# Four products in one half's inverse transform, another split of copies, more input buffers and earlier table loads in a convolution kernel

## The chip, the cores and the metric

The kernel runs on one core of a Trainium2 chip. The metric is the device time of one execution in microseconds (us). Five engines work side by side: PE (TensorE, matrix products), DVE (VectorE), ACT (ScalarE), POOL (GpSimd), and SP, which here only issues transfers (DMAs).

## The reference

Three parts follow each other: a long convolution with a gate, then two feed-forward layers over the 12480 tokens of 128 channels. All is float32.

```python
h_mlp = np.maximum(pos_emb @ w1, 0.0) @ w2            # filter, 12480 x 128
h_filt = h_mlp * np.exp(-0.01 * pos)[:, None]
u = x * v
y = irfft(rfft(u, n=2 * S) * rfft(h_filt, n=2 * S))[:S]   # along the tokens
x = x * y
h = x @ w_in; P = a0 + a1*h + a2*h**2 + a3*h**3; Q = 1 + |b0|*|h| + |b1|*h**2
x = (P / (Q + 1e-06)) @ w_out                         # 128 -> 2048 -> 128
out = np.maximum(0.01 * g, g) @ w_out2, with g = x @ w_in2
```

## The kernel before

The convolution is a Fourier transform over n = n1 * 128 + n2, made of matrix products in two stages, and taken apart into two halves of 64 channels (g = 0 and g = 1). After it come the two feed-forward layers, whose instructions a planner has put in order. The change leaves the planner's part alone; it takes from 400 us to the end of the span. What lies ahead of it runs in this order:

**Filter and u** (to about 106 us). PE, ACT and DVE compute the filter's network; ACT copies it to `hf` (half 0) and by way of DRAM (`hsc`) keeps half 1. In between stand 16 calls of `make_u(c)`: POOL multiplies a chunk of x by one of v (98 x 1024 elements), then DVE makes the sum and the difference of mirrored rows, two instructions of 98 x 512 that write the array `u`. The chunks come through `XB` = 4 buffers for x and `VB` = 2 for v; `load_u` puts the next loads into SP's queue, four DMAs for a chunk of x and four for a chunk of v, two of each four of 192 KB. Each DMA on SP or ACT also waits for an earlier one, since the program's DMAs take eight semaphores in turn.

**First stage, half 0.** `first(g, s, i)`, 16 chunks for the filter (s = 1) and 16 for u (s = 0). A chunk is four products (eight matrix instructions) into one of three PSUM buffers (`ps_b`), and a copy out of it into `A`. ACT copies in three instructions (L644 to L646), except for the chunks that the table `DCH` names for that (g, s): those are copied by DVE in four (L640 to L642). A chunk's products wait until the chunk three before it has been copied. Between the chunks stands `feed(1)`: one step of `conv_all`, which turns the float64 weights of the layers into float32. A weight chunk takes six DVE instructions (L586 to L601), then two on POOL (L605, L608), then a store by SP (`wsc`). Six steps are one weight chunk.

**Second stage, half 0.** 23 blocks. `second(b)`: products `xp` on PE with a table `mt` that SP loads from `c_m`; ACT copies the filter's part (L678); DVE multiplies twice (L685); POOL makes the complex product's parts in `yt`, index 2 and 1 (L691, L692), and their sum, index 0 (L693). Three blocks later `inverse(b)`: three products `gp` with the three tables in `em`, into the single PSUM buffer of `ps_s`; ACT copies the common part to `g1` (L706), DVE adds it to both others into `gs` (L708, two buffers), and SP stores `gs` to DRAM (`bd`). After each block come two steps of `conv_all`.

**First stage and second stage, half 1.** The same for the other 64 channels. The last three inverse blocks of half 0 stand among the first chunks of `first(1, 0, i)`. There too POOL brings half 1 of the filter into `hf` in four copies (L768), and these can't start before the last `bd` stores have read the memory that `hf` shares. The first three tables for half 1 (`early`) are loaded by SP at chunks 13 to 15 of `first(1, 1, i)`.

## Time and profile before

| | |
|---|---|
| median of 3 runs (lowest to highest) | 1721.95 us (1721.27 to 1724.23) |
| the profiled execution: time, span | 1720.13 us, 1718.3 us |
| PE busy in the span | 93% |
| DVE, ACT, POOL busy in the span | 88%, 81%, 83% |
| mean granted TensorE clock | 0.974 of full speed |

The span runs from the first to the last instruction of the profiled execution; 1.8 us of its time lie outside. Times in the rows below are in us from the span's start unless a column says ns.

### The profile page before, as it was taken

What the parts mean: (1) busy time and instruction counts of PE and PEld (TensorE: products, weight loads), DVE (VectorE), ACT (ScalarE), POOL (GpSimd) and SP (SyncE); (2) the same over time, 40 slices, a digit from 0 to 9 for tenths busy, and PEclk for the clock granted to TensorE, in tenths of its full rate; (3) what the DMA queues carried; (4) which work ended last, traced back from release to release, by engine and by line L of the source; (5) the groups of instructions that cost most, each with busy time, mean ns of one, the idle gap of its engine ahead of it and who ended that gap; (6) DMA issues with size and microseconds to landing.
All of it is one profiled execution on the core that took longest, in us unless ns stands there. A gap on an engine that the chain in (4) does not pass through costs nothing.

```text
span 1718.3 us, 21544 instructions
## 1 busy us (share of the span) xinstructions
PE 1604.1 (93%) x6394; PEld 1122.3 (65%) x6394; DVE 1507.3 (88%) x2473; ACT 1385.0 (81%) x2651; POOL 1424.1 (83%) x1209
## 2 busy tenths in 40 slices
PE   7648777987999999999999999999999999999999
PEld 4537667864566666666666666666666666666666
DVE  3488887658999999999999999999999999999992
ACT  4424235337999999999999999999999999999995
POOL 4535772748999999999999999999999999999993
PEclk9969998988999999999999999999999999999999
DMA  6734832761111110111110111110011111010000
GB/s 168 219 120 140 246 132 80 244 172 25 26 30 30 26 30 6 35 30 31 30 26 10 30 30 30 35 27 23 12 30 35 30 31 26 5 30 5 5 5 15
DMA packets 90100, 97.13 MB, mean 57 GB/s; under 512 B 53290, under 2 KB 58416, under 8 KB 89142
## 3 DMA queue, kind: packets, MB, share of 16 engines
q1 hardware_dynamic: 87462, 92.65, 19.8%
q10 hardware_dynamic: 2520, 3.09, 0.6%
q8 instruction: 51, 0.84, 0.2%
q14 instruction: 67, 0.55, 0.1%
HBM read 70.65 MB, written 25.07 MB: 56 GB/s over the span
## 4 chain that ended last, share of the span: by engine, by line
PE 80%; DVE 7%; DMA 5%; POOL 3%; issue 3%; ACT 2%; SPq 0%; ACTq 0%; POOLq 0%; DVEq 0%
PE o1p L964 19%; PE o2p L964 14%; PE h L489 11%; PE h L490 10%; PE h L491 10%; PE yP L919 3%; PE ap L635 3%; PE xp L676 2%; PE gp L702 1%; DMA bd<-wk 1%; PE o2p L491 1%; PE o2p L490 1%; PE o2p L489 1%; DMA hsc<-A 1%; PE oP L1041 1%
## 5 line engine op out<-in xcount | busy, mean ns | idle before, releaser
L1000 POOL TENSOR_TENSOR wk<-wk 128x980 f32<-128x980 f32 (+1 forms) x208 | 471.3, 2266 | 57.3 <-DVE wk L997 55.8
L964 PE MATMUL o1p<-g,wo 128*128 128x490 f32 (+1 forms) x832 | 386.6, 573 | 9.4 <-DVE g L1015 9.1
L991 POOL TENSOR_SCALAR wk<-wk,pars 128x490 f32<-128x490 f32 (+1 forms) x416 | 312.3, 752 | 49.0 <-ACT wk L983 45.2
L1002 DVE SCALAR_TENSOR_TENSOR v<-wk,absb,v 128x490 f32<-128x490 f32 (+1 forms) x416 | 298.7, 718 | 21.4 <-ACT v L985 14.6
L1009 DVE SCALAR_TENSOR_TENSOR v<-v,r 128x490 f32<-128x490 f32 (+1 forms) x416 | 275.1, 663 | 30.1 <-ACT r L1007 27.7
L964 PE MATMUL o2p<-wk,wo 128*128 128x490 f32 (+1 forms) x624 | 299.4, 568 | 0.0
L1005 ACT ACTIVATE rho<-v,cone 128x490 f32<-128x490 f32 (+1 forms) x416 | 279.9, 674 | 7.0 <-DVE v L1002 5.1
L1012 DVE SCALAR_TENSOR_TENSOR v<-v,r 128x490 f32<-128x490 f32 (+1 forms) x416 | 268.7, 662 | 4.3
L997 DVE TENSOR_TENSOR wk<-h,wk 128x490 f32<-128x490 f32 (+1 forms) x416 | 271.6, 653 | 0.5
L985 ACT ACTIVATE v<-h,absb 128x490 f32<-128x490 f32 (+1 forms) x416 | 254.6, 646 | 19.3 <-DVE g L1015 13.4
L1022 ACT ACTIVATE wk<-h 128x490 f32<-128x490 f32 (+1 forms) x416 | 241.9, 582 | 27.2 <-PE h L491 12.5
L1015 DVE TENSOR_TENSOR g<-wk,v 128x490 f32<-128x490 f32 (+1 forms) x416 | 254.0, 650 | 6.6 <-POOL wk L1000 6.1
L1007 ACT ACTIVATE r<-rho 128x490 f32<-128x490 f32 (+1 forms) x416 | 255.9, 617 | 4.5
L489 PE MATMUL h<-zh,wh 128*128 128x490 f32 (+1 forms) x416 | 248.6, 598 | 4.6 <-DVE wk L997 2.6
L983 ACT ACTIVATE wk<-h 128x490 f32<-128x490 f32 (+1 forms) x416 | 239.8, 579 | 15.9 <-PE h L491 12.6
L993 POOL TENSOR_SCALAR wk<-wk,pars 128x980 f32<-128x980 f32 (+1 forms) x208 | 239.0, 1149 | 0.0
L489 PE MATMUL h<-uh,wh 128*128 128x490 f32 (+1 forms) x416 | 226.4, 544 | 2.1 <-ACT wk L1022 1.3
L964 PEld LDWEIGHTS o1p<-g,wo 128*128 128x128 f32 x832 | 156.8, 191 | 105.0 <-issue 49.9
L491 PE MATMUL h<-zh,wl 128*128 128x490 f32 (+1 forms) x416 | 160.4, 386 | 0.0
L490 PE MATMUL h<-zl,wh 128*128 128x490 f32 (+1 forms) x416 | 160.2, 385 | 0.0
L490 PE MATMUL h<-ul,wh 128*128 128x490 f32 (+1 forms) x416 | 159.1, 382 | 0.0
L491 PE MATMUL h<-uh,wl 128*128 128x490 f32 (+1 forms) x416 | 159.0, 382 | 0.0
(100 smaller groups left out, 2522.5 us busy)
## 6 DMA issues: line engine op xcount, KB each, us to landing
bd<-wk SPq DMA_DIRECT2D x44, 256.0 KB
wk<-c_m SPq DMA_DIRECT2D x43, 256.0 KB
bt<-bd SPq DMA_DIRECT2D x96, 112.5 KB
dt<-c_d SPq DMA_DIRECT2D x24, 344.5 KB
A<-x SPq DMA_DIRECT2D x32, 192.0 KB
A<-v SPq DMA_DIRECT2D x32, 192.0 KB
out<-ot SPq DMA_DIRECT2D x32, 192.0 KB
xc<-x SPq DMA_DIRECT2D x24, 240.0 KB
```

Of the source, the lines that this page charges most:

```text
L489: pe.matmul(dst, w_h, z_h, start=start, stop=False)
L490: pe.matmul(dst, w_h, z_l, start=False, stop=False)
L491: pe.matmul(dst, w_l, z_h, start=False, stop=stop)
L964: pe.matmul(o, wo[l][:, f], T.pop((src, n))[:, :w], start=(f == 0), stop=(f == NF - 1))
L991: pool.tensor_scalar(out=q, in0=sq, scalar1=a3, scalar2=a1, op0=ALU.mult, op1=ALU.add)
L997: dve.tensor_tensor(out=half("nn"), in0=one("h1"), in1=two("q"), op=ALU.mult)
L1000: pool.tensor_tensor(out=nn, in0=nn, in1=T["p", n][:, : 2 * w], op=ALU.add)
L1002: dve.scalar_tensor_tensor(out=one("v"), in0=two("s"), scalar=bb, in1=one("v"), op0=ALU.mult, op1=ALU.add)
L1005: act.activation(mk("rho"), one("v"), AF.Abs_reciprocal_sqrt, bias=cone)
L1007: act.activation(mk("r0"), one("rho"), AF.Square)
L1009: dve.scalar_tensor_tensor(out=one("v"), in0=one("v"), scalar=C1, in1=one("r0"), op0=ALU.add, op1=ALU.mult)
L1012: dve.scalar_tensor_tensor(out=one("v"), in0=one("v"), scalar=-2.0, in1=one("r0"), op0=ALU.add, op1=ALU.mult)
```

## The change

Five things. (1) In half 0 the inverse is four products instead of three: real and imaginary part are each the sum of two products in PSUM. The sum `yt` index 0 is not made there (L693), and neither is DVE's addition: ACT copies both parts straight into `gs`. Half 1 keeps the three products; its tables are loaded into `em` between the halves. (2) `DCH` names 15 chunks for DVE instead of 24, so ACT copies 49 of 64. (3) x has six buffers and v four; those for v move to memory that `conv_all` uses later. (4) DVE's sum and difference in `make_u` go through the elements in the order in which x and v lie, and write `u` with a step of 128 elements; before, the reads had that step, and four elements in a row were written. (5) The three early tables are loaded at chunks 0 to 2 of `first(1, 1, i)`.

```diff
-    e = np.stack([np.cos(a), -np.sin(a) - np.cos(a), np.sin(a) - np.cos(a)], axis=1)
+    e = np.stack([
+        np.cos(a), np.sin(a), -np.sin(a), np.cos(a), -np.sin(a) - np.cos(a), np.sin(a) - np.cos(a)
+    ]).reshape(2, 3, N2, N2).transpose(0, 2, 1, 3)
...
-        XB, VB = 4, 2
+        XB, VB = 6, 4
         XS = [cut(Aw, AH + i * 2 * UB * D, [2, UB, D]) for i in range(XB)]
-        VS = [cut(Aw, AH + (XB + i) * 2 * UB * D, [2, UB, D]) for i in range(VB)]
+        VS = [cut(wk, N2 * DG + i * 2 * UB * D, [2, UB, D]) for i in range(VB)]
...
-                dve.tensor_tensor(
-                    out=u[:NU, :, j : j + UB], in0=t[:, 1].rearrange("p n d -> p d n"),
-                    in1=t[:, 0, ::-1].rearrange("p n d -> p d n"), op=alu,
-                )
+                dve.tensor_tensor(out=un[:NU, j : j + UB], in0=t[:, 1], in1=t[:, 0, ::-1], op=alu)
...
-        sp.dma_start(em, I["c_e"])
+        sp.dma_start(em, I["c_e"][0])
...
         DCH = {
-            (0, 1): (4, 6, 8, 10, 12, 14), (0, 0): (1, 4, 6, 9, 11, 14),
-            (1, 0): (1, 4, 6, 9, 11, 14), (1, 1): (1, 4, 6, 9, 11, 14),
+            (0, 1): (9, 12, 15), (0, 0): (2, 6, 10, 14), (1, 0): (2, 6, 10, 14), (1, 1): (2, 6, 10, 14),
         }
...
-                en.tensor_tensor(out=yt[:, 0, :kn], in0=yt[:, 1, :kn], in1=yt[:, 2, :kn], op=ALU.add)
+                if g:
+                    en.tensor_tensor(out=yt[:, 0, :kn], in0=yt[:, 1, :kn], in1=yt[:, 2, :kn], op=ALU.add)
...
-                for r in (2, 1, 0):
-                    pe.matmul(gp[:, r + (r > 0), :kn], em[:, r], yt[:, r, :kn], start=True, stop=True)
+                if g:
+                    for r in (2, 1, 0):
+                        pe.matmul(gp[:, r + (r > 0), :kn], em[:, r], yt[:, r, :kn], start=True, stop=True)
+                else:
+                    for r, es in ((0, (0, 2)), (1, (1, 0))):
+                        for i, e in enumerate(es):
+                            pe.matmul(gp[:, 2 + r, :kn], em[:, e], yt[:, 2 - i, :kn], start=(i == 0), stop=(i == 1))
...
-                    g1 = view("g1", [KB, DG])
-                    act.copy(g1[:, :kn], gp[:, 0, :kn])
                     gs = view("mt" if g and b > NB - 3 else "gs", [KB, 2, DG])
-                    dve.tensor_tensor(
-                        out=gs[:, :kn].rearrange("p k r d -> p r k d"), in0=gp[:, 2:4, :kn],
-                        in1=g1[:, :kn].unsqueeze(1).to_broadcast([128, 2, kn, DG]), op=ALU.add,
-                    )
+                    dst = gs[:, :kn].rearrange("p k r d -> p r k d")
+                    if g:
+                        g1 = view("g1", [KB, DG])
+                        act.copy(g1[:, :kn], gp[:, 0, :kn])
+                        dve.tensor_tensor(
+                            out=dst, in0=gp[:, 2:4, :kn],
+                            in1=g1[:, :kn].unsqueeze(1).to_broadcast([128, 2, kn, DG]), op=ALU.add,
+                        )
+                    else:
+                        act.copy(dst, gp[:, 2:4, :kn])
...
             first(1, 1, i)
+            if i < NE:
+                early[i] = cut(uw, 3072 + 512 * i, [KB, 128])
+                fetch_m(early[i], i)
+            if i == NE:
+                sp.dma_start(em, I["c_e"][1])
             feed(1)
-            if i >= 16 - NE:
-                b = i + NE - 16
-                early[b] = cut(uw, 3072 + 512 * b, [KB, 128])
-                fetch_m(early[b], b)
```

Three places of DVE's program show what moves. The first is the end of `make_u` and the start of its copies in the first stage of half 0; in `ap_1_16` the second number is the channel at which the chunk starts (chunk 4). Before:

```order
5 L476 TENSOR_TENSOR u<-A 98x128x4 x32
6 L640 COPY A<-ap_1_16_612 64x90x4 x2
7 L641 COPY A<-ap_1_16_612 64x90x4
8 L642 TENSOR_SCALAR A<-ap_1_16_612 64x90x4
9 L586 TENSOR_SCALAR wk<-wk 128x512
10 L588 TENSOR_SCALAR wk<-wk 128x512
11 L640 COPY A<-ap_1_24_633 64x90x4 x2
```

The same place in the changed kernel:

```order
5 L479 TENSOR_TENSOR u<-A 98x4x128 x32
6 L586 TENSOR_SCALAR wk<-wk 128x512
7 L588 TENSOR_SCALAR wk<-wk 128x512
8 L591 TENSOR_SCALAR wk<-wk 128x512
9 L595 TENSOR_SCALAR wk<-wk 128x512
10 L597 SCALAR_TENSOR_TENSOR wk<-wk 128x512
11 L640 COPY A<-ap_1_36_663 64x90x4 x2
12 L641 COPY A<-ap_1_36_663 64x90x4
13 L642 TENSOR_SCALAR A<-ap_1_36_663 64x90x4
```

DVE's first copy after u is now chunk 9 instead of chunk 4, and five weight steps stand ahead of it. The second place is three blocks of the second stage of half 0, DVE before:

```order
75 L708 TENSOR_TENSOR wk<-gp_0_944,wk 128x2x4x64
76 L685 TENSOR_TENSOR wk<-xp_3_938,wk 128x512 x2
77 L586 TENSOR_SCALAR wk<-wk 128x512
78 L588 TENSOR_SCALAR wk<-wk 128x512
79 L708 TENSOR_TENSOR wk<-gp_1_967,wk 128x2x4x64
80 L685 TENSOR_TENSOR wk<-xp_4_961,wk 128x512 x2
81 L591 TENSOR_SCALAR wk<-wk 128x512
82 L595 TENSOR_SCALAR wk<-wk 128x512
83 L708 TENSOR_TENSOR wk<-gp_2_988,wk 128x2x4x64
84 L685 TENSOR_TENSOR wk<-xp_5_982,wk 128x512 x2
85 L597 SCALAR_TENSOR_TENSOR wk<-wk 128x512
86 L601 SCALAR_TENSOR_TENSOR wk<-wk 128x512
```

And in the changed kernel:

```order
60 L684 TENSOR_TENSOR wk<-xp_3_934,wk 128x512 x2
61 L586 TENSOR_SCALAR wk<-wk 128x512
62 L588 TENSOR_SCALAR wk<-wk 128x512
63 L684 TENSOR_TENSOR wk<-xp_4_956,wk 128x512 x2
64 L591 TENSOR_SCALAR wk<-wk 128x512
65 L595 TENSOR_SCALAR wk<-wk 128x512
66 L684 TENSOR_TENSOR wk<-xp_5_976,wk 128x512 x2
67 L597 SCALAR_TENSOR_TENSOR wk<-wk 128x512
68 L601 SCALAR_TENSOR_TENSOR wk<-wk 128x512
```

The additions that read `gp` are gone from DVE, and the weight steps keep their places. The third place is DVE at the start of the first stage of half 1 (`ap_0_4`, `ap_0_16` and `ap_0_24` are chunks 1, 4 and 6). Before, from chunk 4:

```order
165 L640 COPY A<-ap_0_16_1442 64x90x4 x2
166 L641 COPY A<-ap_0_16_1442 64x90x4
167 L642 TENSOR_SCALAR A<-ap_0_16_1442 64x90x4
168 L601 SCALAR_TENSOR_TENSOR wk<-wk 128x512
169 L586 TENSOR_SCALAR wk<-wk 128x512
170 L640 COPY A<-ap_0_24_1467 64x90x4 x2
171 L641 COPY A<-ap_0_24_1467 64x90x4
172 L642 TENSOR_SCALAR A<-ap_0_24_1467 64x90x4
173 L588 TENSOR_SCALAR wk<-wk 128x512
174 L591 TENSOR_SCALAR wk<-wk 128x512
175 L595 TENSOR_SCALAR wk<-wk 128x512
176 L640 COPY A<-ap_0_36_1496 64x90x4 x2
```

In the changed kernel, from chunk 6 (`ap_0_24`) to chunk 10 (`ap_0_40`):

```order
125 L597 SCALAR_TENSOR_TENSOR wk<-wk 128x512
126 L601 SCALAR_TENSOR_TENSOR wk<-wk 128x512
127 L586 TENSOR_SCALAR wk<-wk 128x512
128 L640 COPY A<-ap_0_24_1442 64x90x4 x2
129 L641 COPY A<-ap_0_24_1442 64x90x4
130 L642 TENSOR_SCALAR A<-ap_0_24_1442 64x90x4
131 L588 TENSOR_SCALAR wk<-wk 128x512
132 L591 TENSOR_SCALAR wk<-wk 128x512
133 L595 TENSOR_SCALAR wk<-wk 128x512
134 L597 SCALAR_TENSOR_TENSOR wk<-wk 128x512
135 L640 COPY A<-ap_0_40_1480 64x90x4 x2
```

The steps L588 and L591 stood ahead of chunk 9's copy, and now stand, with L595 and L597, ahead of chunk 10's.

## Rows read from the trace of the kernel before

**Rows 1.** Windows: length, busy us (count) of PE, PEld, DVE, ACT, POOL, clock, DMA share, GB/s

```profile
145.00:240.00 95.00, 76.81 (x337) 62.09 (x336) 77.63 (x121) 23.60 (x49) 69.83 (x81) 0.98 0.65 205
297.00:372.00 75.00, 72.36 (x318) 61.73 (x318) 50.54 (x84) 26.64 (x58) 49.60 (x66) 0.96 0.61 207
400.00:1718.00 1318.00, 1298.70 (x4955) 867.14 (x4954) 1233.12 (x2062) 1231.40 (x2346) 1204.72 (x1002) 1.00 0.10 23
```

**Rows 2.** Timeline, 66 to 144 us: start, length, instruction, idle time before and its releaser

```profile
66.49 2.35 POOL L472 TENSOR_TENSOR A<-A 98x1024 f32<-98x1024 f32 x1 [3.18 <-DMA A<-v]
...
78.09 4.48 POOL L472 TENSOR_TENSOR A<-A 98x1024 f32<-98x1024 f32 x1
...
106.32 0.95 DVE L640 COPY A<-ap 64x360 f32<-64x360 f32 x2
...
108.30 0.43 DVE L586 TENSOR_SCALAR wk<-wk 128x512 int32<-128x512 int32 x1
108.33 7.31 PE L635 MATMUL ap<-f1t,wk 128*128 128x180 f32 x32 [27.81 <-DVE A L642]
...
143.71 7.14 PE L676 MATMUL xp<-A,wk 128*128 128x256 f32 x32 [1.72 <-ACT A L646]
```

**Rows 3.** Waits of SP's queue, 34 to 64 us, then 64 to 99: total, times, longest

```profile
SPq L347 <- DMA hsc<-A: 18.2, 10, 6.8
...
SPq L347 <- DVE u L476: 6.1, 4, 2.8
```

**Rows 4.** DVE's line L476, 66 to 107 us: ns shortest/median/longest

```profile
L476 DVE TENSOR_TENSOR u<-A x18: 1114/1222/3186, 68.9 to 105.2; 98x512 f32<-98x512 f32 x18
```

**Rows 5.** Instruction groups up to 374 us: busy us, mean ns, idle before

```profile
L803 DVE TENSOR_TENSOR wl<-w2f,wh 128x512 fp32r<-128x512 f32 x8 | 5.5, 681 | 0.0
...
L708 DVE TENSOR_TENSOR wk<-gp,wk 128x512 f32<-128x512 f32 x44 | 30.1, 687 | 16.9 <-ACT wk L706 9.0 <-DMA bd<-wk 7.5
...
L644 ACT COPY A<-ap 64x720 f32<-64x720 f32 x40 | 30.1, 752 | 74.4 <-PE ap L635 70.6 <-DMA hsc<-A 3.4
...
L646 ACT ACTIVATE A<-ap 64x360 f32<-64x360 f32 x40 | 18.6, 465 | 0.0
L645 ACT COPY A<-ap 64x360 f32<-64x360 f32 x40 | 18.1, 454 | 0.5
```

**Rows 6.** Timeline of PE, second stage: half 0 three and six blocks on, then half 1

```profile
168.53 1.53 PE L702 MATMUL gp<-wk,em 128*128 128x256 f32 x6 [0.27 <-DVE wk L708]
...
179.98 1.53 PE L702 MATMUL gp<-wk,em 128*128 128x256 f32 x6 [0.27 <-DVE wk L708]
...
314.74 1.89 PE L676 MATMUL xp<-A,wk 128*128 128x256 f32 x8
...
316.47 1.46 PE L702 MATMUL gp<-wk,em 128*128 128x256 f32 x6
...
317.76 1.89 PE L676 MATMUL xp<-A,wk 128*128 128x256 f32 x8
```

**Rows 7.** Waits, 143 to 236 us: total, times, longest

```profile
PE gp L702 <- DVE wk L708: 17.8, 16, 3.6
...
DVE wk L708 <- DMA bd<-wk: 7.5, 6, 3.6
```

**Rows 8.** DMA traffic, 172 to 215 us

```profile
DMA packets 4302, 10.61 MB, mean 247 GB/s; under 512 B 496, under 2 KB 496, under 8 KB 3973
```

**Rows 9.** Timeline, 238 to 300 us, first stage of half 1

```profile
239.34 0.94 PE L702 MATMUL gp<-wk,em 128*128 128x128 f32 x6
...
244.16 7.82 POOL L768 COPY wk<-u 82x2048 f32<-82x2048 f32 x2 [9.87 <-DMA bd<-wk]
...
257.91 3.95 DVE L591 TENSOR_SCALAR wk<-wk 128x512 int32<-128x512 int32 x1
...
264.34 7.59 PE L635 MATMUL ap<-f,u 98*128 98x180 f32 x32 [3.71 <-DVE A L642]
...
297.41 2.90 PE L676 MATMUL xp<-A,u 128*128 128x256 f32 x6 [3.96 <-DMA u<-c_m]
```

More of the change, by code (lines that the diff above doesn't have):

```diff
@@ L407, in conv_moe_moe @@
         un = u.rearrange("p d n -> p n d")
-        rh = cut(Aw, AH + 3 * 2048, [N2 // 2, NH])
+        rh = cut(Aw, AH + 6 * 1024, [N2 // 2, NH])
         pos = cut(Aw, 0, [N2, FO])
```

## The prediction

> **What bounds the kernel now.** I read the windows first, cut by stage. From 400 us on PE is busy for 1298.7 of 1318 us at the full granted clock [rows 1]; the change touches nothing there, so that part stays. Everything that can move lies ahead of it. In the second stage of half 0 PE is at 76.8 of 95 us and DVE at 77.6, in that of half 1 PE is at 72.4 of 75 [rows 1]: the same work is set by PE in half 1 and by something else in half 0. Then I followed the chain that ends each stage in the timeline, which gives four stretches.
>
> *u.* POOL starts chunk 7 at 66.49, and DVE is done with the last chunk and turns to the first copy at 106.32 [rows 2]. A lone product on POOL takes 2.35 us; the one at 78.09, which starts while DVE works on the chunk before, takes 4.48 [rows 2]. DVE's instruction takes 1.11 us at its shortest and up to 3.19 [rows 4]. So the two hold each other up: nine chunks in 39.83 us are 4.43 each, about 2.35 + 2 x 1.11 = 4.57. They run one behind the other all the way, and PE stands idle for 27.8 us behind them [rows 2], because the copy of chunk 4 is queued on DVE behind u.
>
> *First stage, half 0.* From 108.33 to the first `xp` at 143.71 [rows 2] it does 25 chunks, 1.415 us each.
>
> *Second stage, half 0.* 143.71 [rows 2] to the last `gp` at 239.34 [rows 9], 95.6 us. In its steady part three blocks take 179.98 - 168.53 = 11.45 us, 3.82 a block; a block of half 1 takes PE 1.73 us (`xp`) and 1.29 (`gp`), 3.02 [rows 6]. PE waits 17.8 us for DVE's addition L708, and that in turn 7.5 us for the store of the buffer it writes to [rows 7]: DVE is the bound, the stores add to it.
>
> *First stage, half 1.* 239.34 to 297.41, 58.1 us. POOL's copies start at 244.16; meanwhile DVE's weight steps, such as L591 at 257.91, take 3.95 us where L586 alone takes 0.43 [rows 2, 9]. Chunk 6 waits on DVE behind them, so PE goes on with chunk 9 only at 264.34. At the end PE waits 3.96 us for the early tables [rows 9].
>
> **The change part by part.**
>
> *Buffers for x and v.* I cost them at nothing. Between 34 and 64 us SP waits for no buffer, only for DMAs ahead, 18.2 us of it for stores of `hsc` [rows 3]; more buffers leave that as it is. After 64 us it waits 6.1 us for DVE to free one [rows 3], but that is hidden under POOL and DVE, which are the bound there. If that cover goes, loads have to bring 4 x 192 KB = 0.79 MB a chunk, 3.2 us at the 247 GB/s of [rows 8].
>
> *The new order of DVE's sum and difference.* No row shows a DVE write of single elements 512 bytes apart. With operands that lie in order, 128x512 from SBUF takes 0.681 us (L803, [rows 5]), against 1.114 for L476. The copy L640 writes runs of four elements, 512 bytes apart, at 0.95 / 2 = 0.475 us for 360 elements [rows 2], no slower per element than L803, so the steps between runs cost nothing. I take 0.681, since the strided reads are what sets L476 apart from both. Two instructions in nine chunks: 9 x 2 x 0.433 = 7.8 us. A chunk then takes 3.56 us, just above the 3.2 of the loads. Bounds: 0 if writes with that step cost what such reads do, 9 x (4.43 - 3.2) = 11 if only the loads were left. u ends at 98.5.
>
> The Trainium skill (Advanced Engine Details and Errata, SBUF Cachelines) says that accesses which move to another 16-byte line each time are penalised, and names no difference of reads and writes. L476's reads agree with it, at 1.114 against 0.681 us. By that rule the new writes, one element to a line, would keep the instruction near 1.11 us, and the 7.8 us would fall away.
>
> *Copies in the first stage of half 0.* ACT now takes chunks 0 to 8 before u is done, which needs 9 x (0.752 + 0.454 + 0.465) = 15 us [rows 5], well inside PE's 27.8 us of idling. After u, DVE has five weight steps (5 x 0.43 = 2.2 us), then chunk 9 (106.32 to 108.30, 1.98 us [rows 2]), and PE resumes at chunk 12 with 20 left: 2.2 + 2.0 + 20 x 1.415 = 32.5, against 143.71 - 106.32 = 37.4. Gain 4.9. ACT has three chunks in four, 5.0 us for 4 x 1.415 = 5.7. Bounds 3 (steps held up by the weight load) to 8 (1.27 us a chunk, the rate after 264.34, below).
>
> *Four products.* PE pays 1.29 / 3 = 0.43 us more a block: 1.73 + 1.72 = 3.45. DVE loses L708, 0.687 us [rows 5]: 11.45 - 3 x 0.687 = 9.4 us for three blocks, below PE's 10.35. POOL loses one of three instructions. ACT copies 512 instead of 256 elements a block, hidden: it was busy 23.6 of 95 us [rows 1]. So PE becomes the bound. 22.5 blocks (the last is half) x 3.45 = 77.6, and three first-stage chunks in between at 1.27 are 3.8: 81.4 against 95.6, at best 14.2. Transfers take some of it back: 172 to 215 us moves 10.61 MB at 247 GB/s [rows 8], and at PE's pace (3.45 for about 4.1 us a block) that would need 290. I take 3 us off: gain 11.2. Lower bound 5: that stretch stays as it is, and the other 52.6 us shrink by 1 - 10.35 / 11.45.
>
> *Copies in the first stage of half 1.* DVE has L597, L601 and L586 before POOL's copies start, then chunk 6 in time; L588 needs POOL's L608, which stands behind two of the four copies, so chunk 10 now takes the place that chunk 6 had, behind the copies. PE does four chunks more before it stops there, and resumes at chunk 13 instead of 9. From 264.34 to the end of the products (297.41 - 3.96 = 293.45) 23 chunks took 1.27 us each [rows 9]; so 4 x 1.27 = 5.1, less 0.7 for L597, the one step more ahead of the copy. Gain 4.4; bounds 2 and 10, where the copies collide otherwise.
>
> *Early tables.* They leave SP's queue behind chunks 0 to 2, ahead of the last two weight stores. PE waits 3.96 us for them, of which the copy of the last chunk (1.67 us, L644 to L646 [rows 5]) stays: gain 2.3. The half's `em` goes out with them, a dozen chunks before it is read, and costs nothing; were it late, the first `gp` of half 1 would wait.
>
> Sum: 7.8 + 4.9 + 11.2 + 4.4 + 2.3 = 30.6 us. The profiled execution took 1720.13, span 1718.3 and 1.8 around it, so 1689.5; the median of the runs is 1.8 above that execution, which gives 1691.4.
>
> **The rivals.**
>
> *Writes cost as reads did* (the rule above, as a mechanism of this kernel): u again ends near 106.3, and 22.8 us are left: 1699. For it: the nearest row has runs of four, not single elements. Against: L640 shows no cost of its writes.
>
> *Transfers bound the second stage of half 0.* `gs` has two buffers; DVE already waits 7.5 us for their stores [rows 7], and at 3.45 us a block the time for a store to land shrinks from 8 to 7 us. Then ACT waits in L708's place and holds PE's single `gp` buffer. Against: half 1 runs at 3.02 with the same buffers and 207 GB/s [rows 1, 6]. It leaves the lower bound: 1720.13 - 30.6 + 6.2 + 1.8, 1698; with the rival above, 1705.
>
> *Slower.* The new writes are far dearer than the reads. Place: L479, 18 instructions after 66 us, each with POOL kept out. From (1.11 + 22.8 / 18) = 2.4 us for one, twice what it takes now, they eat all other gains; at 3 us the kernel is at about 1733. For it: no row with such writes. Against: the slowest undisturbed access here is 1.114.
>
> *The change doesn't do what it says:* the deeper buffers load nothing earlier, as [rows 3] show for 34 to 64 us. That is in the sum already.
>
> **How the numbers follow.** Likeliest, 0.5: 1691.4, own range 1684 to 1698. Writes as dear as reads, 0.26: 1699. Transfers, 0.12: 1698; both, 0.05: 1705. Slower, 0.03: 1733. Better than 1683 (bounds of several terms at once), 0.04. The range 1683 to 1706 leaves out the last two and the edges. 0.2% is 3.4 us, about what a measurement can tell from no change: faster 0.95, the same 0.02, slower 0.03.
>
> **What would show it.** L479 near 0.68 us, and DVE's first copy near 98.5. First `xp` near 131. In half 0's second stage `gp` to `gp` 3.45 us with PE busy throughout; waits there for a `bd` store speak for the transfers. POOL's copies still stretch L588 and L591, and PE resumes at chunk 13 right after. The first `xp` of half 1 follows ACT's last copy, not a DMA. The prediction is wrong if L479 stays above 1 us, or if the 1318 us of the layers move.

## The result, and the profile after

The changed kernel takes 1696.38 us (median of 4 runs, 1694.75 to 1704.04) against 1721.87 for the kernel before, measured beside it: a ratio of 0.9858, 95% interval [0.9827, 0.9889]. It is 25.5 us faster. 1691.4 was forecast, with a range of 1683 to 1706. The profiled execution took 1696.18 us, with a span of 1694.4, 23.9 less than before.

The timeline of the changed kernel gives the marks that cut the 23.9 us into stages (start, length, instruction, idle time before and its releaser):

```profile
67.43 2.35 POOL L475 TENSOR_TENSOR A<-A,wk 98x1024 f32<-98x1024 f32 x1 [3.01 <-DMA wk<-v]
...
89.38 1.49 PE L635 MATMUL ap<-f1t,wk 128*128 128x180 f32 x8 [1.68 <-ACT A L646]
92.54 1.49 PE L635 MATMUL ap<-f1t,wk 128*128 128x180 f32 x8 [1.68 <-ACT A L646]
...
103.06 0.41 DVE L586 TENSOR_SCALAR wk<-wk 128x512 int32<-128x512 int32 x1
...
107.00 2.77 PE L635 MATMUL ap<-f,u 98*128 98x180 f32 x8 [12.97 <-DVE A L642]
111.74 7.94 PE L635 MATMUL ap<-f,u 98*128 98x180 f32 x32 [1.98 <-DVE A L642]
120.14 13.98 PE L635 MATMUL ap<-f,u 98*128 98x180 f32 x88 [0.46 <-ACT A L646]
135.84 7.14 PE L675 MATMUL xp<-A,wk 128*128 128x256 f32 x32 [1.72 <-ACT A L646]
...
169.40 1.89 PE L707 MATMUL gp<-wk,em 128*128 128x256 f32 x8
...
172.85 1.89 PE L707 MATMUL gp<-wk,em 128*128 128x256 f32 x8
...
223.72 1.06 PE L707 MATMUL gp<-wk,em 128*128 128x128 f32 x8
...
227.32 7.66 POOL L777 COPY wk<-u 82x2048 f32<-82x2048 f32 x2 [10.37 <-DVE wk L601]
...
240.85 3.86 DVE L591 TENSOR_SCALAR wk<-wk 128x512 int32<-128x512 int32 x1
...
247.79 6.94 PE L635 MATMUL ap<-f,u 98*128 98x180 f32 x24 [10.52 <-DVE A L642]
254.57 20.26 PE L635 MATMUL ap<-f1t,wk 128*128 128x180 f32 x128
276.51 5.45 PE L675 MATMUL xp<-A,u 128*128 128x256 f32 x24 [1.68 <-ACT A L646]
...
283.52 1.46 PE L703 MATMUL gp<-wk,em 128*128 128x256 f32 x6
```

On PE, x8 of L635 is one chunk of a first stage; `f1t` marks the filter's chunks and `f,u` those of u. Five marks of each kernel do for the whole study: POOL's chunk 7 (67.43 here), the end of u (DVE's next step, 103.06), the first `xp` (135.84), the last `gp` of half 0 (223.72, the 128x128 one), and the first `xp` of half 1 (276.51). Before, they stood at 66.49, 106.32, 143.71, 239.34 and 297.41 [rows 2, 9]. Differences of such marks, from the timeline of each kernel's profiled execution, in us:

| kernel | chunk 7 to end of u | to first `xp` | to last `gp` | to `xp` of half 1 | to the end |
|---|---|---|---|---|---|
| before | 39.83 | 37.39 | 95.63 | 58.07 | 1420.89 |
| changed | 35.63 | 32.78 | 87.88 | 52.79 | 1417.89 |
| changed, once more (e11) | 35.85 | 32.05 | 88.86 | 51.95 | 1418.51 |
| e1 u in a row | 32.01 | 32.02 | 91.61 | 52.05 | 1418.73 |
| e2 three `gs` | 36.07 | 32.20 | 87.15 | 52.86 | 1420.98 |
| e3 steps later | 35.44 | 32.00 | 87.86 | 47.91 | 1418.49 |
| e4 late tables | 36.31 | 33.02 | 89.88 | 53.44 | 1420.52 |
| e5 old order of u | 39.02 | 32.65 | 87.52 | 52.90 | 1419.20 |
| e6 old buffers | 36.81 | 33.33 | 87.62 | 53.25 | 1419.03 |
| e7 three products | 35.68 | 32.85 | 95.37 | 52.86 | 1418.98 |
| e8 old split of copies | 35.62 | 37.99 | 89.21 | 55.65 | 1418.49 |
| e9 filter on ACT | 35.88 | 25.41 | 87.75 | 52.60 | 1418.64 |
| e10 strided weights | 32.92 | 38.43 | 89.08 | 52.81 | 1419.85 |
| e12 together | 36.02 | 25.89 | 81.44 | 47.60 | 1421.03 |

Chunk 7 itself starts anywhere from 65.50 to 67.43 us in the nine kernels that make u as the changed one does; that is noise, and the columns leave it out. (Four experiments act on the chunks before it too: it starts at 66.88 us in e1, 64.81 in e5, 66.36 in e6 and 68.51 in e10.) Where kernels share a stage, the rows differ by up to 1.3 us in the first stages and 2.4 in the second (e1 more, see there).

Of the 23.9 us, u gives 3.3 (4.2 in its column, less 0.9 for a later chunk 7), half 0's first stage 4.6, its second stage 7.75, the first stage of half 1 5.3, and the time behind it 3.0.

The windows of the changed kernel, with their columns as in [rows 1]:

```profile
107.00:116.70 9.70, 7.72 (x24) 7.26 (x25) 7.91 (x16) 3.15 (x6) 2.80 (x3) 0.50 0.34 117
136.00:224.00 88.00, 82.29 (x383) 70.92 (x383) 64.85 (x96) 28.94 (x51) 55.53 (x60) 1.00 0.69 222
224.00:277.00 53.00, 40.75 (x241) 39.36 (x241) 35.43 (x59) 35.04 (x67) 25.63 (x14) 0.87 0.26 87
247.79:254.57 6.78, 6.78 (x24) 6.78 (x25) 3.36 (x8) 1.58 (x3) 1.44 (x1) 0.54 0.47 166
380.00:1694.00 1314.00, 1297.18 (x4952) 866.42 (x4950) 1230.19 (x2056) 1229.30 (x2340) 1201.35 (x998) 1.00 0.10 23
255.00:274.00 19.00, 18.96 (x123) 18.41 (x122) 13.72 (x28) 18.17 (x35) 6.48 (x6) 1.00 0.24 81
276.50:283.50 7.00, 6.99 (x32) 6.19 (x33) 2.58 (x4) 1.75 (x3) 2.19 (x4) 1.00 0.24 68
```

In the second stage of half 0 PE is now busy for 82.3 of 88 us and DVE for 64.9; before it was 76.8 and 77.6 of 95 [rows 1]. The layers, from 380 us on, are as they were. The waits of that second stage (135 to 225 us; engine, line, what it waited for: total, times, longest):

```profile
ACT wk L720 <- DMA bd<-wk: 18.3, 6, 4.6
...
PE gp L707 <- ACT wk L720: 3.7, 3, 2.5
```

DVE's wait for stores (7.5 us [rows 7]) has become ACT's, and grown to 18.3; PE waits for ACT only 3.7 us of the stage.

### The profile page after: what moved, and what is told of

It reads as the page before. It is cut to its first block, busy times and chain, and to the rows that moved or that the text cites. A ratio compares the mean times of both kernels' runs of the same rounds, so it can differ in the third digit from the quotient of the medians.

```text
span 1694.4 us, 21566 instructions
## 1 busy us (share of the span) xinstructions
PE 1606.8 (95%) x6440; PEld 1127.9 (67%) x6440; DVE 1471.7 (87%) x2413; ACT 1403.8 (83%) x2678; POOL 1404.7 (83%) x1191
## 4 chain that ended last, share of the span: by engine, by line
PE 77%; DVE 3%; ACT 1%; POOL 1%; issue 1%; DMA 0%; SPq 0%; DVEq 0%; ACTq 0%; POOLq 0%
PE o1p L974 19%; PE o2p L974 14%; PE h L489 11%; PE h L491 10%; PE h L490 10%; PE yP L929 3%; PE xp L675 2%; PE gp L703 2%; PE o2p L491 1%; PE o2p L490 1%; PE o2p L489 1%; PE oP L1051 1%; DVE v L1012 1%; DVE g L1025 1%; PE xP L922 1%
## 5 line engine op out<-in xcount | busy, mean ns | idle before, releaser
L1019 DVE SCALAR_TENSOR_TENSOR v<-v,r 128x490 f32<-128x490 f32 (+1 forms) x416 | 275.1, 663 | 29.5 <-ACT r L1017 27.1
```

Source lines behind the costliest of these rows:

```text
L1019: dve.scalar_tensor_tensor(out=one("v"), in0=one("v"), scalar=C1, in1=one("r0"), op0=ALU.add, op1=ALU.mult)
```

## The experiments

Each kernel is the changed one with the edit shown. The kernels of a group ran on one chip beside the kernel before, which took 1723.76 us for e1 to e4, 1720.04 for e5 to e8, 1723.97 for e9 to e11 and 1721.28 for e12. The yardstick e11 is the changed kernel itself. Distances to it are given by the ratios; the kernel before was 3.9 us quicker in the group of e5 to e8 than in that of e11, so by plain medians these four lie 3.9 us closer to it. The columns of the table lie between the two and decide.

**e11, the changed kernel once more.**

> The changed kernel as it is, as a yardstick on the same chip for the others of this call. Expected: 0.9858 of the kernel before within its interval, 0.983 to 0.989. Should it come out at 0.9835 or less, the run with three gs buffers gained nothing and the one with late tables lost more than its ratio told; at 0.988 or more, the undone parts cost less than told.

1697.27 us (1696.34 to 1699.23), ratio 0.9851 [0.9837, 0.9866]. The first measurement holds, with a narrower interval.

**e5, the old order of DVE's sum and difference.** The deleted statement of the change's diff in place of the new one.

> The changed kernel with DVE's old order in make_u: reads 512 bytes apart, four elements written in a row. Theory, the order gives what the two durations differ by, 1.11 against 1.02 us at their shortest: 18 x 0.09 = 1.6 us, u ends at 104 to 105.5, the time is 1698. Rival, the order gives nothing and the 3.3 us by which u ends earlier come from the buffers: u ends at 103 and the time stays at 1696.4. The prediction's reading (7.8 us from the order) would put u's end at 106 or later and the time above 1700.

1698.38 us (1697.81 to 1698.97), ratio 0.9877 [0.9863, 0.9892], some 4.5 us (0.0026) above the yardstick, with intervals that just overlap. DVE's line in this kernel (ns shortest/median/longest):

```profile
L479 DVE TENSOR_TENSOR u<-A x32: 1096/1216/3209, 24.5 to 102.7; 98x512 f32<-98x512 f32 x32
```

In the changed kernel the same row is

```profile
L479 DVE TENSOR_TENSOR u<-A x32: 1015/1046/3173, 26.1 to 102.2; 98x512 f32<-98x512 f32 x32
```

The new order saves 0.17 us an instruction, 18 x 0.17 = 3.1 us for nine chunks, and the table shows 39.02 against 35.63, 3.4. So DVE's instruction still lies on the path that bounds u, and the writes, one element every 512 bytes, cost nearly what the reads did. The end of u itself shows less: it is at 103.83 us here and at 100.94 to 103.13 in the nine kernels with the new order and buffers, because chunk 7 starts early here.

**e1, u written in a row.** This leaves out the transposition: u's columns land elsewhere, so its products are of other data.

```diff
-                dve.tensor_tensor(out=un[:NU, j : j + UB], in0=t[:, 1], in1=t[:, 0, ::-1], op=alu)
+                dve.tensor_tensor(
+                    out=cut(uw, (16 * q + c) * UB * D, [UB, D])[:NU], in0=t[:, 1], in1=t[:, 0, ::-1], op=alu
+                )
```

> The changed kernel, but DVE's sum and difference write their 512 elements one behind the other (u then holds its columns in another order, so the output is another one; the work and the waits are the same). Theory 1, a write of single elements 512 bytes apart costs DVE about as much as such a read, 1.05 us an instruction against 0.68: L479 falls to about 0.68 us. What that gives depends on what bounds u. 1a, POOL and DVE excluding each other still bound it: u ends at 98.5 to 99.5 instead of 103.1, and the time falls by about 4 us to 1692. 1b, the loads have become the bound (POOL waits 10.4 us for x and v in the changed kernel's last nine chunks): u ends at 101 to 102, the time falls by 1 to 2. Rival, the half rate has another cause than the write's step (two operands with a turned order, for instance): L479 stays near 1.05 us and the time near 1696.

1691.78 us (1690.85 to 1695.07), ratio 0.9822 [0.9803, 0.9841], 5 us (0.0029) below the yardstick. DVE's line:

```profile
L479 DVE TENSOR_TENSOR u<-A x32: 678/688/2869, 26.0 to 98.3; 98x512 f32<-98x512 f32 x32
```

With reads and writes both in a row it takes 0.688 us, and u ends at 98.89, chunk 7 to end 32.01, 7.0 us less than in e5. That is what the prediction asked of the new order (0.681 us, 7.8 us, end at 98.5). DVE's time does reach the end of u, though POOL still waits 8.4 us for x and v around these chunks; what was not to be had with the real layout was the 0.681 us. Of the 4.9 us that e1 gains by the first `xp` (130.91 against 135.84) its profiled execution kept only 1.2 at the last `gp`. The first `xp` of it, and two windows behind it:

```profile
130.91 8.83 PE L677 MATMUL xp<-A,wk 128*128 128x256 f32 x32 [1.72 <-ACT A L648]
```

```profile
131.00:140.00 9.00, 9.00 (x34) 7.63 (x35) 5.20 (x9) 1.94 (x4) 4.64 (x6) 0.81 0.57 173
145.00:195.00 50.00, 44.82 (x191) 37.80 (x190) 36.52 (x53) 13.73 (x24) 32.52 (x35) 0.93 0.82 255
```

A granted clock of 0.81 and 0.93, where the changed kernel has 1.00 from 136 to 224, is part of that; the profiled execution is also the slowest of its four, and why the clock fell there is left open.

**e10, the step moved from DVE's writes to PE's weight loads.** u lies in two halves of 64 channels, so DVE writes runs of 64 elements, and PE loads columns whose elements are 256 bytes apart.

```diff
-        un = u.rearrange("p d n -> p n d")
+        uh = uw.rearrange("p (g n d) -> p g n d", g=2, n=N2)
+        ug = uw.rearrange("p (g n d) -> p n g d", g=2, n=N2)
...
-                dve.tensor_tensor(out=un[:NU, j : j + UB], in0=t[:, 1], in1=t[:, 0, ::-1], op=alu)
+                dve.tensor_tensor(
+                    out=ug[:NU, j : j + UB], in0=t[:, 1].rearrange("p n (g d) -> p n g d", g=2),
+                    in1=t[:, 0, ::-1].rearrange("p n (g d) -> p n g d", g=2), op=alu,
+                )
...
-                lhs = hf[:, c + i_] if s else u[:NU, g * DG + c + i_]
+                lhs = hf[:, c + i_] if s else uh[:NU, g, :, c + i_]
```

> The changed kernel with u laid out so that VectorE writes runs of 64 elements, and PE's weight loads read it with 256 bytes from element to element instead. Theory 'writes with a step cost as reads do': L479 (here some lines on) falls from 1.046 to 0.69 us, u ends 3 to 4.5 us earlier as in the run with u in a row. If PE's reads of weights cost no more with a step than without, loads of u stay at 190 ns, the first xp comes 4 us earlier and the time is 1692 to 1693. Rival 'the cost moves with the step': the 256 loads of u take twice their 190 ns or more; at 380 ns they no longer hide beside a product's 316 ns, each of 32 chunks costs 8 x 0.064 = 0.5 us more, 16 us in all: 1708. At 1.05 us a load (what VectorE's instruction of 512 columns takes) it would be 32 x 8 x 0.73 = 188 us more.

1701.81 us (1699.21 to 1704.38), ratio 0.9873 [0.9852, 0.9894]: 4.5 us above the yardstick, with intervals that overlap. PE in the first stages, the filter's products, then the loads and products of u:

```profile
L639 PE MATMUL ap<-f1t,wk x256: 315/316/667, 65.5 to 279.8; 128*128 128x180 f32 x128
L639 PEld LDWEIGHTS ap<-f,u x256: 291/313/333, 105.4 to 259.4; 98*128 98x128 f32 x128
L639 PE MATMUL ap<-f,u x256: 317/383/670, 105.4 to 259.6; 98*128 98x180 f32 x128
```

The same row of u's loads in the unchanged kernel (e11):

```profile
L635 PEld LDWEIGHTS ap<-f,u x256: 186/190/338, 107.1 to 253.7; 98*128 98x128 f32 x128
```

A load takes 313 ns instead of 190, no longer hidden beside a product (383 instead of 316): the gain of 3 us in u's column is lost twice over in the next one (38.43 against 32.05); the column of half 1 is as it was (52.81). The rival was right in kind, at 6.4 us instead of 16, the lower of its prices.

**e6, the old numbers of buffers.**

```diff
-        XB, VB = 6, 4
+        XB, VB = 4, 2
```

> The changed kernel with four x and two v buffers as before (the v buffers stay in their new place). By the prediction the buffers give nothing: u ends at 103 and the time stays at 1696.4. Rival, they give part of the 3.3 us by which u ends earlier, since SP's waits for DVE and POOL after 64 us (10.1 us before, 0.2 in the changed kernel) made POOL wait for v: u ends at 104 to 106, the time is 1697.5 to 1699.

1697.4 us (1696.64 to 1698.37), ratio 0.987 [0.9854, 0.9887]. The interval overlaps the yardstick's; u's column shows 36.81 against 35.4 to 36.3 in the nine kernels with the new order and the new buffers. By that column the buffers are worth 0.5 to 1.4 us.

**e7, three products in half 0.** Products, tables, POOL's sum and DVE's addition as before, the rest as changed.

```diff
-                if g:
+                if True:
                     for r in (2, 1, 0):
                         pe.matmul(gp[:, r + (r > 0), :kn], em[:, r], yt[:, r, :kn], start=True, stop=True)
```

> The changed kernel with the inverse of half 0 in three products again, with the sum on POOL and DVE's addition (em is loaded once, as before). By the working of the prediction (11.2 us, 7.75 measured for the stage) half 0's second stage is back at 95 to 97 us and the time at about 1704 to 1706. Rival, part of that stage's gain comes from elsewhere (the stages around it start earlier or later against the weight steps): it takes 90 to 93 us and the time is about 1700.

1704.66 us (1704.51 to 1708.44), ratio 0.9919 [0.9904, 0.9934]: 0.0068 above the yardstick, 11.7 us. In the profiled execution the second stage takes 95.37 us, as before the change, and these waits are back in it (135 to 225 us):

```profile
PE gp L703 <- DVE wk L715: 15.8, 15, 3.5
...
DVE wk L715 <- DMA bd<-wk: 6.0, 7, 3.5
```

So the four products alone give 6.5 to 7.5 us of the stage (95.37 less 88.86 and 87.88), or 5.5 to 7.9 against all that this column shows for kernels with the same second stage (e1 left out). The spans of the profiled executions differ by 8.2 us (1702.7 - 1694.5), the medians by 7.4.

**e2, a third buffer for `gs`.**

```diff
-"g1": (256, 2), "gs": (512, 2)
+"g1": (256, 1), "gs": (512, 3)
```

> The changed kernel with three gs buffers instead of two (and one g1 buffer instead of two, which only half 1 uses). Theory, the stores of gs hold up the second stage of half 0, where ACT waits 18.3 us for them: from the first xp to the last gp it takes 81 to 84 us instead of 87.9, the time falls by 4 to 6 us to about 1691. Rival 1, the transfers themselves are the limit: the waits move to the loads of c_m or stay with the third buffer, and the stage stays at 87 to 88. Rival 2, POOL's parts of yt are what PE waits for: the same, with PE waiting for POOL. The single g1 buffer may cost half 1 up to 1 us if ACT has to wait for DVE.

1696.03 us (1694.07 to 1696.67), ratio 0.9841 [0.9824, 0.9859], not to be told from the yardstick. ACT's waits for stores fall from 18.3 us to

```profile
ACT wk L720 <- DMA bd<-wk: 5.7, 2, 4.3
```

and PE no longer waits for ACT at all. Yet the stage is 87.15 us. PE's timeline shows one stop instead, ahead of products that take twice their 1.89 us, and then, at the start of the layers, a longer wait for input than the changed kernel's 4.87 us:

```profile
187.34 3.75 PE L675 MATMUL xp<-A,wk 128*128 128x256 f32 x8 [3.07 <-DMA wk<-c_m]
...
352.04 0.89 PE L922 MATMUL xP<-ident,xc 98*128 98x98 f32 x4 [6.43 <-DMA xc<-x]
```

The windows of the stretch behind that stop:

```profile
186.00:200.00 14.00, 12.66 (x45) 10.70 (x46) 10.53 (x15) 3.52 (x6) 9.51 (x10) 0.76 1.04 328
```

The DMA engines are busy without a pause (a share of 1.04, 328 GB/s) and the clock is 0.76. With the buffer to spare PE ran ahead until a table came late, as the rival on transfers had it: one more buffer only moves the wait. What made the table late is not separated. The transfers are one candidate; the other is the order of SP's queue, in which loads of tables stand behind stores of weights, and these wait for POOL's last weight step. SP's waits over the stage, and its queue just ahead of PE's stop:

```profile
SPq L618 <- POOL wk L608: 24.3, 8, 3.4
```

```profile
179.98 0.32 SPq L618 DMA_DIRECT2D wsc<-wk  x1
...
181.23 0.35 SPq L658 DMA_DIRECT2D wk<-c_m  x1
```

The later input shows in e12 too (6.57 us), which has the same two buffer counts, and in no other kernel (4.86 to 5.40); by it and what follows, the last column is 2.5 us longer. Which of the two counts does it was not tried.

**e8, the old split of copies.**

```diff
-            (0, 1): (9, 12, 15), (0, 0): (2, 6, 10, 14), (1, 0): (2, 6, 10, 14), (1, 1): (2, 6, 10, 14),
+            (0, 1): (4, 6, 8, 10, 12, 14), (0, 0): (1, 4, 6, 9, 11, 14),
+            (1, 0): (1, 4, 6, 9, 11, 14), (1, 1): (1, 4, 6, 9, 11, 14),
```

> The changed kernel with 24 chunks copied by DVE and 40 by ACT, as before. By the prediction 4.9 us are lost behind u (PE resumes at chunk 7 instead of 12) and 4.4 us in half 1's first stage (PE stops at chunks 7 and 9 instead of 13): about 1705. Rival, in half 1 both splits lose the same to POOL's copies and to the clock behind them, so that only the first part counts: about 1701.

1704.67 us (1701.47 to 1707.05), ratio 0.9913 [0.9896, 0.993], 10.7 us (0.0062) above the yardstick. PE's timeline shows the old stop behind u again:

```profile
104.56 7.91 PE L635 MATMUL ap<-f1t,wk 128*128 128x180 f32 x32 [23.29 <-DVE A L642]
```

Its first-stage columns are 37.99 and 55.65, against 32.78 and 52.79: the split gives 5.2 us in half 0 and 2.9 in half 1 (4.7 to 6.0 and 2.4 to 3.7 against all rows with the new split and nothing else changed there).

**e9, the filter's copies all on ACT.**

```diff
-            (0, 1): (9, 12, 15), (0, 0): (2, 6, 10, 14), (1, 0): (2, 6, 10, 14), (1, 1): (2, 6, 10, 14),
+            (0, 1): (), (0, 0): (6, 10, 14), (1, 0): (2, 6, 10, 14), (1, 1): (2, 6, 10, 14),
```

> The changed kernel with all 16 filter chunks of half 0's first stage copied by ScalarE (the table names no chunk for VectorE there, and chunks 6, 10 and 14 of u). Theory 'the queue behind u': of the 32.8 us from the end of u to the first xp, PE stops 12.97 us ahead of chunk 12 only because chunk 9's copy stands on VectorE behind u. With nothing of the filter there, all 16 chunks are done before u ends; what is left is 16 chunks of 1.415 us, 22.6, and the copy of the last, 1.7: 24.3 to 25 us, first xp 8 us earlier, and the second stage keeps its 87.9 us, since the stores and loads in it cost it little: time about 1688.5 us where the unchanged one gives 1696.4. Rival 'given back to the transfers': the first xp comes 8 us earlier, but the second stage, which starts with loads that are no earlier, grows by 4 us or more, and ScalarE waits more than 18.3 us for the stores: 1692 or more. Rival 'the weight steps': twelve steps of the weights, 5.2 us, now stand together on VectorE behind u, so chunk 6 of u waits; first xp only 4 us earlier: 1692, with PE idle ahead of chunk 9 of u.

1690.48 us (1687.7 to 1691.97), ratio 0.9809 [0.9792, 0.9825]: 6.8 us better than the yardstick. PE goes on with u as soon as u is there:

```profile
101.90 18.41 PE L635 MATMUL ap<-f,u 98*128 98x180 f32 x96 [12.73 <-DVE wk L586]
...
126.91 7.14 PE L675 MATMUL xp<-A,wk 128*128 128x256 f32 x32 [1.72 <-ACT A L646]
```

From the end of u to `xp` are 25.41 us, and the second stage keeps its 87.75, with 17.8 us of waiting for stores on ACT: nothing is given back to the transfers. PE still stands for 12.73 us, but only until u is there: it goes on 0.4 us after the end of u (101.50), in the changed kernel 3.9 us after it (107.00), and the second stop of 1.98 us is gone. The queue on DVE behind u was what it waited for beyond that.

**e3, weight steps out of the way of POOL's copies.**

```diff
-            if i >= 3:
+            if i >= 11:
                 feed(1)
         for i in range(16):
             first(1, 1, i)
...
-            feed(1)
+            feed(2 if i < 8 else 1)
```

> The changed kernel with the weight steps of the first eleven chunks of half 1's first u stage given out later: none up to chunk 10, then one a chunk, and two a chunk in the first eight chunks of the filter's stage. Theory, chunk 10's copy waits only because weight steps stand ahead of it on DVE, which wait for POOL behind its copies of the filter: PE's stop of 10.5 us ahead of chunk 13 goes, and with it the slow clock behind it (6.9 us for three chunks instead of about 3.9), so half 1's first stage takes 39 to 42 us instead of 52.8 and the time falls by 10 to 14 us to about 1684. Rival, the filter's stage then waits for POOL's copies (four of 3.8 us from about 227), or the steps that are put off hold up DVE's copies there: 3 to 6 us at most.

1691.54 us (1689.13 to 1694.2), ratio 0.9822 [0.9801, 0.9844], 5 us (0.0029) below the yardstick; from the last `gp` to `xp` are 47.91 us instead of 51.95 to 52.79. The theory's 10 to 14 us and 39 to 42 us did not come; the rival's 3 to 6 us did. PE's timeline has no stop of 10.52 us; the longest of those left is

```profile
239.75 2.53 PE L635 MATMUL ap<-f1t,wk 128*128 128x180 f32 x8 [1.74 <-POOL wk L777]
```

It is the rival's: the filter's stage waits for POOL's copies. Behind it the clock is low again (0.56), and three more stops, of 0.87, 1.54 and 1.22 us, wait for chunks that DVE copies:

```profile
239.75:247.50 7.75, 6.88 (x25) 6.45 (x26) 6.19 (x12) 3.15 (x6) 4.57 (x4) 0.56 0.52 147
```

**e4, the early tables back at chunks 13 to 15.** The fifth part of the change's diff undone (its `em` load stays).

> The changed kernel with the three early tables loaded at chunks 13 to 15 again, as before (the half's em stays where the change put it). By the prediction's term PE waits 2.3 us more at the start of half 1's second stage, and the time is about 1698.7. Theory now, the wait also lets the granted clock fall, so that the first products of that stage run at half speed as they did before (10.0 us from the first xp to the first gp against 7.0): 5.3 us, 1701.7. Rival, the tables arrive in time anyway because the weight stores ahead of them come earlier now: no change, 1696.4.

1698.29 us (1695.98 to 1701.74), ratio 0.9858 [0.9837, 0.9879]. The times don't tell it from the yardstick; the trace does:

```profile
279.38 8.28 PE L675 MATMUL xp<-A,u 128*128 128x256 f32 x24 [3.18 <-DMA u<-c_m]
```

The same 24 instructions take 5.45 us in the changed kernel. The window behind that stop, with a granted clock of 0.71:

```profile
279.40:289.30 9.90, 9.90 (x33) 8.20 (x34) 2.58 (x4) 1.76 (x3) 3.36 (x5) 0.71 0.30 96
```

The wait is 1.5 us longer than ACT's 1.68, and the lower clock costs 2.8 us more (9.84 from `xp` to `gp` against 7.01). Before the change the same stretch took 10.0 us (297.41 to 307.40), in this window:

```profile
297.40:307.40 10.00, 9.99 (x32) 8.29 (x33) 2.58 (x4) 1.76 (x3) 3.34 (x5) 0.69 0.30 92
```

**e12, what the runs point to, together.** The edits of e2, e3 and e9, and eight weight steps fewer in the second stage of half 0.

```diff
-            if i >= 4:
+            if i >= 2:
                 feed(1)
...
-            if i % 4:
-                feed(1)
+            feed(1)
...
             run(st, 1)
-            feed(2)
+            feed(1 if 9 <= b < 17 else 2)
```

> The changed kernel with what the earlier runs point to: all filter chunks of half 0 copied by ScalarE, three gs buffers, the weight steps out of the way of GpSimd's copies in the first stage of half 1, and eight weight steps fewer in blocks 9 to 16 of half 0's second stage, where the DMA queues are full (six of them go to its first stage, two come from the slack at the end). Theory 'separate queues, added up': 6.8 us for the filter chunks and 5 us for the later steps against the unchanged kernel of the same call (0.9851 of before), and in the second stage, with neither a store to wait for nor a load that comes late, PE close to its busy time: 84 us instead of 87.9, 3.5 us. Sum 15: 0.976 of before, some 1682 us where before takes 1724. Rival 'the transfers bind': the stage's bytes hardly change, so it stays at 87 us or above, with waits for a c_m load or a bd store in place of those removed: 0.978 to 0.979. Rival 'the steps come due elsewhere': the six steps put into the first stage of half 0 hold up VectorE's copies of u's chunks, and the first xp comes 2 us or more later than the 25.4 us after u's end of the run with ScalarE's filter copies: 0.979 or more.

1679.53 us (1678.18 to 1680.49), ratio 0.9755 [0.9742, 0.9768]: 42 us faster than before, and 0.0096 (16.5 us) better than the yardstick. Two marks of its timeline and the window of its second stage:

```profile
127.63 7.14 PE L675 MATMUL xp<-A,wk 128*128 128x256 f32 x32 [1.72 <-ACT A L646]
...
209.07 1.06 PE L707 MATMUL gp<-wk,em 128*128 128x128 f32 x8
```

```profile
150.00:200.00 50.00, 49.52 (x230) 43.18 (x228) 34.75 (x53) 16.97 (x29) 33.10 (x39) 1.00 0.85 264
```

The second stage takes 81.44 us, with PE busy for 49.5 of 50. Neither the third buffer alone (87.15) nor the earlier start (e9, 87.75) did that; with the weight steps taken out of blocks 9 to 16, no table comes more than 0.48 us late. The sum of the expectation came out (0.976 expected, 0.9755 measured). The stage moves 18.48 MB here and 19.56 in the changed kernel, and SP waits for L608 about as long as in e2 (22.8 us, seven times).

## Why the prediction was right, and where its sizes were off

The direction holds, and so does the mechanism of most parts. But the 30.6 us were worked out for the profiled execution, and there 23.9 were measured (25.5 on the medians); two stages were misread; and the prediction's own sign of being wrong, L479 above 1 us, came up (1.046). That the time is only 5 us off the forecast is in part luck: 3.0 us that no step had make up for some of what is missing, and 1696.38 lies nearer to the rival's 1699 than to 1691.4. Undone one at a time, by the columns and against the changed kernel's first row, the parts give 3.4 (e5), 1.2 (e6), 5.2 and 2.9 (e8), 7.5 (e7) and 3.3 us (e4, in its last two columns), 23.5 of the 23.9; each carries the 1 to 2 us by which like rows differ.

*The order of u: 7.8 forecast, 3.4 measured (e5).* The failed step is the price of L479. I took 0.681 us from L803, and argued from L640 that steps between writes cost nothing. L640 writes runs of four; with single elements it is 1.046. The rival "writes cost as reads did" was nearly right (1.046 against 1.216), as was its rule: the Trainium skill (Advanced Engine Details and Errata, SBUF Cachelines) penalises accesses that change the 16-byte line each time, and names no difference of reads and writes. e1 and e10 agree with it: with runs of 64 elements or more DVE takes 0.688 us. That what DVE saves reaches the end of u was right: e1 ends u where the sum had it. That POOL and DVE run one behind the other all the way is too strong: at their shortest, nine chunks would take 9 x 2.35 + 18 x 1.015 = 39.4 us in the changed kernel, and they took 35.63.

*The buffers: 0 forecast; 0.5 to 1.4 us (e6).*

*First stage of half 0: 4.9 forecast, 4.6 measured, 5.2 in e8.* The wait for chunk 9's copy is right (3.9 us behind u, 4.2 forecast). The count of what is left behind it is not, and that the size came out is luck. A chunk doesn't always wait for the chunk three before it. In the changed kernel the filter's last two chunks each wait for ACT's copy of the one just before (the stops of 1.68 us at 89.38 and 92.54), while chunks 9 and 12 still wait for DVE: so all 16 chunks of the filter are done when PE stops. At 107.00 it goes on with u's first chunk, 16 left (x8, x32 and x88), not with chunk 12 and 20 left. Before, 23 were left and not 25: seven of the filter, the x32 of [rows 2] and

```profile
116.09 2.71 PE L635 MATMUL ap<-f1t,wk 128*128 128x180 f32 x16 [0.46 <-ACT A L646]
119.25 1.49 PE L635 MATMUL ap<-f1t,wk 128*128 128x180 f32 x8 [0.46 <-ACT A L646]
120.58 1.39 PE L635 MATMUL ap<-f,u 98*128 98x180 f32 x8
```

The 16 chunks took 27.1 us, 1.70 each instead of 1.415: the clock was 0.50 from 107.00 to 116.70, and PE stood 1.98 us more for chunk 12's copy. e9 has neither chunk on DVE and gains 6.6 us in this column over e11.

*Four products: 11.2 forecast, 7.75 measured, 7.5 in e7.* `gp` to `gp` is 3.45 us where nothing waits (169.40 to 172.85), exactly PE's own time; DVE is off the path. The failed step is the 3 us taken off for the transfers: 6.5 us stand between 87.9 and the 81.4 of the sum. PE is busy for 82.2 of the 87.9 and stands for 5.6, 3.7 of them for ACT and 1.9 for POOL; but e2, where it never waits for ACT, is only 0.7 shorter, less than like rows differ by. e12 reaches 81.44. It changes the start, the buffers and the weight steps together; as the first two alone gave next to nothing, the steps in the blocks where the queues are full, by their transfers or by their place in SP's queue, are the likeliest cause. That is argued: the weight steps alone were not tried.

*First stage of half 1: 4.4 forecast, 2.9 measured (e8).* PE does stop at chunk 13 behind POOL's copies, and L591 does take 3.86 us beside them. The stop ends 24.1 us behind the last `gp` (25.0 before), 0.9 earlier instead of 0.7 later. The failed step is the reading of [rows 9]. The row at 264.34 is x32 of u, four chunks, so PE went on with chunk 12 there, not 9; before that it had stopped ahead of chunk 9, for chunk 6's copy (kernel before):

```profile
254.40 6.23 PE L635 MATMUL ap<-f,u 98*128 98x180 f32 x24 [6.80 <-DVE A L642]
```

So 20 chunks were left in the 29.1 us to 293.45, not 23, at 1.46 us each and not 1.27; and the new split moves the last stop by one chunk, from 12 to 13, not by four. From 247.79 to 274.83 (276.51 less 1.68) the nineteen that are left take 27.0 us: three of them 6.8 at a clock of 0.54, and sixteen 20.3, 1.27 each, with PE busy for 18.96 of 19 us. 0.9 and 2.1 us make 3.0; e8 shows 2.9.

*Early tables: 2.3 forecast, 2.4 measured at the `xp` (58.07 to 55.65 in e8, which has the early tables and the old split), and 3.0 more behind it that no step had.* PE no longer idles for 3.96 us there, and its clock stays at 1.00 where it was 0.69; e4 loses 2.0 to 2.6 of those 3.0 again (1420.52 against 1418.51 and 1417.89); the column itself differs by 2.0 between like kernels, but the 2.8 us behind e4's `xp` are seen directly.

The last column of the table is otherwise untouched, as forecast. The slower case did not come near: no L479 took longer than 3.2 us, and the median fell.

## What to carry to other kernels

When a copy with a step is moved from the reads to the writes of an instruction, look for a row with the same run length, not only the same step: runs of four said nothing of single elements. Before a stretch is divided by a number of chunks, count them in the rows: x32 was four chunks where the order of the source suggested seven. Engines that work through queues wait for what stands ahead: here 6.8 us were to be had by giving the copies behind a late input to another engine, and 5 by moving fillers away from a stretch where they run at a ninth of their speed. And when one wait is removed in a stage whose transfers are near full, look at everything else that goes through the queue: one more buffer alone gained nothing here, and the kernel that also moved eight weight steps away came down to PE's own time.

## What the runs showed of the hardware that was not expected

Writes of single elements 512 bytes apart cost DVE 1.046 us for 512 columns, against 0.688 in a row and 1.216 for reads with that step. PE's weight loads, too, pay for a step: 313 ns against 190 with 256 bytes between elements. A wait of PE of a few us can have a second price: in e4, behind 3.18 us of waiting, the granted clock was 0.71 on the mean of the next 9.9 us (part of them at 1.2 GHz, part at 2.4) and cost 2.8 us; in the changed kernel, behind 1.68 us, it stayed at 1.00. The length of that last wait alone doesn't settle it: in e1 the clock was 0.81 in the nine us behind a wait of 1.72.
